# Chunks 4 to 8 cut into columns of 32 tokens, their q loaded by GpSimd during the first unit and turned by VectorE

## The chip, the core and the metric

The kernel runs on one core of a Trainium2 chip. Its parts in this text: TensorE (PE, matmuls; PEld is its weight load), VectorE (DVE), ScalarE (ACT), GpSimd (POOL) and SyncE (SP, which issues DMAs). The metric is the device time of the kernel in microseconds (us): 909.27, the median of three runs (908.77 to 909.46).

## The reference

An attention block without a softmax, then a two-layer block on its output:

```python
kv  = einsum('bhsd,bhse->bhde', k, v)          # 8 batches, 8 heads, 576 tokens, 64 wide
o   = einsum('bhsd,bhde->bhse', q, kv)
x   = o / sqrt(mean(o*o, -1) + 1e-6) * g_norm  # per token and head
x   = x.transpose(0, 2, 1, 3).reshape(4608, 512)
r   = maximum(x @ w_in, 0)                     # 512 -> 2048
out = (s * (r * r) + b) @ w_out                # 2048 -> 512
```

All is float32 but w_in and w_out, which come as 64-bit floats and are made float32 on the chip.

## The kernel before

**Chunks, pairs, units.** The 4608 tokens are cut into 36 chunks of 128 tokens, four chunks make one of nine units of 512 tokens, and from chunk 4 on the attention is worked out for two chunks at a time (c and c+1, c even). A chunk need not be 128 tokens in a row: `parts(c)` (L119) says which. Two cuts exist. In the first nine chunks (two batches) a batch is seen as 64 rows of 9 columns, token = 9p + j, and a chunk is two columns of 64 tokens. In the others a batch is seen as 32 rows of 18 columns, token = 18t + j, and a chunk is four columns of 32 tokens. The output rows follow the same cut: `store` (L1206) issues one DMA for each column, so two for a chunk of the first kind (64 rows) and four for one of the second (32 rows).

**Loading and turning q.** TensorE needs q with the head's 64 numbers on the partitions. For a chunk of the first kind `load_q` (L131) issues two DMAs on the queues it is given (SP in all calls that matter here), which put tokens on the partitions; `turn` (L518) then has TensorE transpose it in four instructions (L534) into PSUM and ScalarE copy it out (L535). For a chunk of the second kind the DMAs themselves bring each 32-token column of each head and half head to its block, 16 DMAs for each run of neighbouring columns, issued by GpSimd (L1623 in the profile); VectorE then turns the 32 x 32 blocks, a whole pair in one instruction (L524), or one chunk of it (L530) where the pair is mixed, as chunks 8 and 9 are. The steps after that are `product` (L545), `back` (L557), `square`, `row_sum`, `norm` (L578), `turn_x` (L589) and `scale`. The q tiles have two buffers, so the load of chunks 8 and 9 goes where chunks 4 and 5 were.

**The order of the work** is written out by hand. In unit 0 twelve plain blocks of the first layer run (`first_unit`, L1633), with the conversion of the weights' 1 MB blocks beside them (`raw` on ScalarE, `convert` on VectorE, three raw buffers); then the fourth part of the layer by a seven-product scheme (`mm1`: x1, z2, x6, y7, x5, x3, y4), then the second layer in 14 slots (`mm2`). The attention of the next unit is put between these: `side_of` (L1590) gives the steps beside the second layer, by slot number, and `sides` (L1680) those beside the first layer; A is the first pair of the next unit, B the second. `at(n)` runs the steps of place n. An engine works through its instructions in the order in which they are written, so a step that waits holds what is written after it on the same engine.

**DMA issue.** SP issues the weights, k and v, and the stores of derived weights to DRAM (`store_w2`, L315). GpSimd issues the output stores, the stores of sums of w_out (L1110) and the q loads of the second kind. `of_w` holds the two halves of `sums_w_in(3)` (L253 and L250): sums of weights that y7, x5 and later products of unit 0 read.

Of the kernel before, what the change touches and what calls it, by code (L numbers as in the profile page):

```python
# [9 lines left out]
FP32 = mybir.dt.float32  # L10
# [6 lines left out]
def kernel(  # L17
# [39 lines left out]
    nc = tc.nc  # L57
# [60 lines left out]

    def parts(c):  # L119

        g, i = divmod(c, R)
        if g == 0:
            if i == 4:
                return [(0, 8, 1), (1, 8, 1)]
            b, i = (0, i) if i < 4 else (1, i - 5)
            return [(b, i, 1), (b, 4 + i, 1)]
        if i == 4:
            return [(2 * g, 16, 2), (2 * g + 1, 0, 2)]
        return [(2 * g, 4 * i, 4)] if i < 4 else [(2 * g + 1, 4 * i - 18, 4)]

    def load_q(c, queues=(nc.sync, nc.sync), rest_on=nc.gpsimd):  # L131

        t = qp.tile([P, 2 * DM], FP32, name="q_sb", tag="q")
        q_tile[c] = t
        pieces = []
        for i in range(2):
            if c + i < R:
                q_in[c + i] = t[:, i * DM : i * DM + DM].rearrange("p (h d) -> p h d", h=H)  # L140
        for s, queue in enumerate(queues):
            for i in range(2):
                if c + i < R:
                    b, j, _ = parts(c + i)[s]
                    queue.dma_start(
                        out=q_in[c + i][s * HB : s * HB + HB],
                        in_=q[b].rearrange("h (p j) d -> p j h d", j=R)[:, j],
                    )
        for i in range(2):
            if c + i < R:  # L150
                continue
            w = 4 * i
            for b, j, n in parts(c + i):
                if pieces and pieces[-1][1] == b and pieces[-1][2] + pieces[-1][3] == j:
                    pieces[-1][3] += n
                else:
                    pieces.append([w, b, j, n])
                w += n
            q_in[c + i] = t.rearrange("p (a w) -> p a w", a=NP)[:, :, i * P : i * P + P]
            if c + i == R:  # L160
                q_in[R] = t[:, DM:].rearrange("p (a w) -> p a w", a=NP)
        rest = []
        for w, b, j, n in pieces:
            src = q[b].rearrange("h (t j) d -> h t j d", j=JC)
            to = t.rearrange("p (a w d) -> p a w d", a=NP, d=32)
            if c < R:
                to, w = t[:, DM:].rearrange("p (a w d) -> p a w d", a=NP, d=32), 0
            for h in range(H):
                for a in range(2):
                    rows = slice(32 * (2 * (h % 2) + a), 32 * (2 * (h % 2) + a) + 32)  # L170
                    rest.append(
                        partial(
                            rest_on.dma_start,
                            out=to[rows, h // 2, w : w + n, :],
                            in_=src[h, :, j : j + n, a * 32 : a * 32 + 32],
                        )
                    )
        return rest
# [319 lines left out]
    def attention_of_two(c):  # L498
# [16 lines left out]
        W = 8  # L515
        st = {}

        def turn(i=None):  # L518
            if i in (None, 0):
                st["qT"] = attp.tile([P, 2 * DM], FP32, name="qT", tag="qT").rearrange(  # L520
                    "p (a x) -> p a x", a=NP
                )
            if i is None:
                nc.vector.transpose(  # L524
                    out=st["qT"], in_=q_tile[c].rearrange("p (a x) -> p a x", a=NP)
                )
                return
            to = st["qT"][:, :, i * P : i * P + P]
            if c + i >= R:
                nc.vector.transpose(out=to, in_=q_in[c + i])  # L530
                return
            ps = ps_t.tile([P, NP, P], FP32, name="qT_ps", tag="t")
            for p in range(NP):
                nc.tensor.transpose(ps[:, p, :], q_in[c + i][:, 2 * p : 2 * p + 2, :], ident)  # L534
            nc.scalar.copy(to, ps)  # L535

        def product():
            ps = [ps_t.tile([P, 2, 2 * P], FP32, name="y_ps", tag="t") for _ in range(2)]
# [123 lines left out]
    def g_s1(s):  # L662
        add(ga["s1", s], ga["a21", s], ga["a22", s])
# [404 lines left out]
    def mm2(u, step=None, side={}):  # L1068
# [135 lines left out]
            return st[name, j]  # L1204

        def store(name, j, c, cols=slice(0, DM), queues=(nc.gpsimd, nc.gpsimd)):  # L1206
            view = out_9 if c < R else out_18
            w = view.shape[2]
            for s, (b, jj) in enumerate((b, jj + i) for b, jj, n in parts(c) for i in range(n)):
                queues[s % 2].dma_start(  # L1210
                    out=view[b, jj, :, cols], in_=st[name, j][s * w : s * w + w, cols]
                )
# [377 lines left out]
    def side_of(A, B, sums, u):  # L1590

        if u == 0:
            return {
                6: [lambda: kv_product(1)],
                7: [partial(A["turn"], 0), partial(A["turn"], 1)],
                8: [A["product"], A["back"], A["square"]],
                9: [A["row_sum"], partial(B["turn"], 0), partial(B["turn"], 1)],
                10: [A["norm"], A["turn_x"], A["scale"], B["product"], B["back"], B["square"]],
                11: [B["row_sum"], B["norm"]],
                12: [B["turn_x"], B["scale"], lambda: [fn() for fn in sums_w_in(0)]],  # L1600
                13: [sums],
            }
        of_w_in = [
            partial(sums_of_w_in, *with_tags)
            for with_tags in zip(DEEP, ((5, 6), (7, 4), (5, 6)))
        ]
        return {
            0: [A["scale"]],
            1: [B["turn"]],
            4: [B["product"], B["back"], B["square"]],  # L1610
            5: [B["row_sum"]],
            6: [B["norm"], of_w_in[1]],
            8: [B["turn_x"], B["scale"], of_w_in[2]],
            11: [sums],
            13: [partial(loads, 3, 1)],
            3: [of_w_in[0]],
        }

    def loads(u, i):

        if u < U:
            for load in load_q(4 * u + 2 * i):
                load()  # L1623

    def raw(i):
        hi(i)
        lo(i)
# [5 lines left out]
    def first_unit():  # L1633
        of_x = x_sums(0)
        of_w = []

        for n, slot in enumerate(slots0):
            if n > 1:
                out_of = slot()
                if out_of:  # L1640
                    out_of()
                if n % 4 == 0:
                    g_s1(n // 4 - 1)
            if 0 < n < 9:
                raw(n + 2)
                convert(n + 2)
            elif n == 0:
                continue
            elif n == 9:
                of_w += sums_w_in(3)  # L1650
                of_w[0]()
            elif n == 10:
                of_x[0]()
                raw(11)
                of_x[1]()
            else:
                of_w[1]()
            if n < 11:
                scale_g()
            if n == 9:  # L1660
                more(8)
        a = mm1(0, NS - 1)
        for fn in (
            a["x1"], scale_g, partial(convert, 11), partial(more, 9),
            a["z2"],
            a["x6"], partial(raw, 12), scale_g, partial(g_s1, 2),
            a["y7"], partial(convert, 12),
            a["x5"], partial(raw, 13), scale_g, partial(more, 10), partial(more, 11),
        ):
            fn()  # L1670
        return a
# [8 lines left out]
    def sides(u, A, B):  # L1680
# [9 lines left out]
        if u == 1:  # L1690
            for s in range(1, NS - 1):
                first[((0, 1), (0, 3))[s - 1]] = list(sums_w_in(s))
            first.update({
                (1, 3): kv,
                (2, 0): [partial(A["turn"], 0), partial(A["turn"], 1)],
                (2, 1): [A["product"]],
                (2, 2): [A["back"]],
                (2, 3): [A["square"]],
                (3, 0): [A["row_sum"]],
                (3, 2): [A["norm"], A["turn_x"]],  # L1700
                (3, 3): [lambda: [load() for load in load_q(12, rest_on=nc.sync)]],
            })
            return first, second
# [39 lines left out]
    for u in range(U):  # L1743
# [38 lines left out]
        for n, slot in enumerate(second):  # L1782
            slot()
            if u == 0:
                if n == 0:
                    convert(13)
                    load_kv(1, 0, convp, tag="raw", bufs=3)
                    store_w2(1, 5)
                    for name in ("x3", "y4", "y4_square"):
                        last[name]()  # L1790
                    raw(14)
# [2 lines left out]
                elif n == 1:  # L1794
                    convert(14)
                    load_kv(1, 1, convp, tag="raw", bufs=3)
                    raw(15)
                    loads(1, 0)
                    loads(1, 1)
                elif n == 2:  # L1800
                    convert(15)
                    t2 = convp.tile([P, 4 * R * D], FP32, name="w_t2", tag="raw", bufs=3)
# [43 lines left out]
```

## Time and profile before

| | |
|---|---|
| median of the three runs | 909.27 us |
| the profiled execution's own time | 909.36 us |
| its span, first to last instruction | 907.6 us |
| TensorE busy | 897.1 us, 99% |
| VectorE busy | 667.2 us, 74% |
| ScalarE busy | 357.5 us, 39% |
| GpSimd busy | 227.6 us, 25% |
| TensorE's waits for another engine or a DMA | 6.5 us, in eleven waits |
| q loads by GpSimd (L1623), issue time | 256, 143.7 us |
| turns by TensorE (L534) | 20, 2.7 us |
| turns of a pair by VectorE (L524) | 13, 1236 ns each |

Times inside the execution count from the span's start. The chain of waits is the path of work that ended last, followed back through what released each step. A timeline lists an engine's instructions with their start, their length and the idle time before them.

### The profile page before, as it was taken

Reading aid. Unit: us, or ns where it says so; the run is one execution under the profiler, and the core shown is the slowest. Engines: PE = TensorE matmul, PEld = TensorE weight load, DVE = VectorE, ACT = ScalarE, POOL = GpSimd, SP = SyncE. Lnnn points to the kernel's source line nnn. Section 1 sums busy time; section 2 is a strip of 40 time slices with the busy share of each in tenths; the row PEclk is TensorE's granted clock in tenths of the full one; section 3 lists DMA queues with packets and bytes.
Section 4 is the critical chain, followed back from the end, with each engine's and each line's share of the span. In section 5 each row is a group of like instructions: output and inputs, shape, how many; then the busy total and the mean of one; then the engine's idle time right before and its main releaser. Section 6 shows DMA issues by size and latency. Waiting matters only on the chain.

```text
span 907.6 us, 19247 instructions
## 1 busy us (share of the span) xinstructions
PE 897.1 (99%) x7514; PEld 824.9 (91%) x7514; DVE 667.2 (74%) x1234; ACT 357.5 (39%) x603; POOL 227.6 (25%) x432
## 2 busy tenths in 40 slices
PE   7999999999999999999999999999999999999998
PEld 7888888888889998999899998999899989999998
DVE  2889576587567986878678857885878777874686
ACT  2887134531148115630365026701680057104710
POOL 2000017014623233811283026503440300021000
PEclk9999999999999999999999999999999999999999
DMA  9695968239943894379626972598438811891285
GB/s 255 221 319 173 280 159 242 84 90 397 334 135 84 282 328 140 79 246 315 188 72 191 308 246 77 128 306 259 126 94 287 287 36 53 278 305 47 56 258 184
DMA packets 120138, 180.34 MB, mean 199 GB/s; under 512 B 29168, under 2 KB 46320, under 8 KB 120048
## 3 DMA queue, kind: packets, MB, share of 16 engines
q1 hardware_dynamic: 101552, 153.00, 53.7%
q0 software_dynamic: 15040, 23.88, 8.8%
q10 hardware_dynamic: 3456, 2.23, 1.0%
q8 instruction: 60, 0.98, 0.4%
q14 instruction: 30, 0.25, 0.1%
HBM read 153.36 MB, written 25.69 MB: 197 GB/s over the span
## 4 chain that ended last, share of the span: by engine, by line
PE 89%; DVE 5%; ACT 2%; DMA 2%; issue 1%; ACTq 0%; DVEq 0%
PE x_ps L91 46%; PE y_ps L91 26%; PE z_ps L91 9%; PE sx_ps L91 4%; PE y_ps L545 2%; DMA kv_sb<-in_v_dram 1%; PE kv_ps L366 1%; DMA w_raw<-in_moe_w_in_dram 1%; ACT w_raw L230 1%; PE z_ps L366 1%; ACT w_raw L225 1%; DVE xs L253 1%; DVE xn L578 0%; DVE a L253 0%; DVE w_up L245 0%
## 5 line engine op out<-in xcount | busy, mean ns | idle before, releaser
L1623 POOL DMA_DIRECT2D q_sb<-in_q_dram x256 | 143.7, 570 | 133.9 <-ACT a L652 62.6
L1210 POOL DMA_DIRECT2D out_dram<-o x110 | 54.8, 505 | 395.8 <-issue 153.0
L91 PE MATMUL x_ps<-w_sb,sub 128*128 128x128 f32 x1176 | 148.8, 275 | 0.6 <-DVE r L250 0.6
L91 PEld LDWEIGHTS x_ps<-w_sb,sub 128*128 128x128 f32 x1176 | 139.7, 192 | 0.9 <-DVE r L250 0.9
L644 ACT ACTIVATE a<-a,b_col,s_col 128x512 f32<-128x512 f32 x144 | 116.2, 813 | 29.6 <-DVE a L647 23.2
L91 PE MATMUL x_ps<-xs,ws 128*128 128x256 f32 x528 | 125.2, 380 | 0.1
L91 PE MATMUL y_ps<-xs,wb 128*128 128x256 f32 x528 | 124.6, 381 | 0.2 <-DVE wb L253 0.2
L91 PEld LDWEIGHTS y_ps<-xs,wb 128*128 128x128 f32 x528 | 97.5, 190 | 13.3 <-issue 0.6
L91 PEld LDWEIGHTS x_ps<-xs,ws 128*128 128x128 f32 x528 | 96.9, 190 | 12.1 <-ACT r L718 0.5
L819 ACT COPY a<-x_ps 128x512 f32<-128x512 f32 x28 | 16.4, 584 | 216.2 <-PE x_ps L91 216.0
L91 PE MATMUL x_ps<-xT,wa 128*128 128x256 f32 x360 | 83.7, 381 | 0.1
L91 PEld LDWEIGHTS x_ps<-xT,wa 128*128 128x128 f32 x360 | 66.7, 190 | 10.3 <-issue 1.5
L250 DVE TENSOR_TENSOR r<-sx_ps,a 128x256 f32<-128x256 f32 x63 | 26.6, 422 | 62.2 <-PE sx_ps L91 62.1
L91 PE MATMUL x_ps<-w_sb,a 128*128 128x128 f32 (+1 forms) x432 | 64.9, 298 | 0.0
L91 PE MATMUL y_ps<-w_sb,a 128*128 128x128 f32 (+1 forms) x416 | 62.1, 295 | 0.0
L91 PEld LDWEIGHTS x_ps<-w_sb,a 128*128 128x128 f32 x432 | 58.9, 191 | 3.3 <-issue 0.4
L91 PEld LDWEIGHTS y_ps<-w_sb,a 128*128 128x128 f32 x416 | 56.1, 192 | 2.1
L250 DVE TENSOR_TENSOR a<-y_ps,r 128x512 f32<-128x512 f32 x38 | 26.1, 688 | 37.7 <-PE y_ps L91 30.0
L250 DVE TENSOR_TENSOR r<-x_ps,o 128x256 f32<-128x256 f32 (+1 forms) x84 | 29.7, 353 | 29.3 <-PE x_ps L91 28.6
L91 PE MATMUL y_ps<-w_sb,sub 128*128 128x128 f32 x392 | 49.5, 275 | 0.0
L253 DVE TENSOR_TENSOR a<-a,a 128x512 f32<-128x512 f32 x72 | 46.8, 684 | 0.4
L91 PE MATMUL z_ps<-w_sb,a 128*128 128x128 f32 (+1 forms) x352 | 46.8, 280 | 0.0
(185 smaller groups left out, 1519.6 us busy)
## 6 DMA issues: line engine op xcount, KB each, us to landing
w_sb<-w SPq DMA_DIRECT2D x385, 256.0 KB, 4.4
w_raw<-in_moe_w_in_dram SPq DMA_DIRECT2D x8, 1024.0 KB, 7.8
w_raw<-in_moe_w_out_dram SPq DMA_DIRECT2D x8, 1024.0 KB, 5.0
w_sb<-w SPq DMA_DIRECT2D x14, 512.0 KB, 8.8
w<-sub POOLq DMA_DIRECT2D x28, 256.0 KB, 6.5
w_sb<-in_k_dram SPq DMA_DIRECT2D x24, 288.0 KB, 4.8
w_sb<-in_v_dram SPq DMA_DIRECT2D x24, 288.0 KB, 5.0
out_dram<-o POOLq DMA_DIRECT2D x92, 64.0 KB, 4.0
```

The lines of the kernel that those rows point to most:

```text
L91: nc.tensor.matmul(o, lhsT=lhsT, rhs=rhs, start=start, stop=stop, skip_group_check=True)
L225: nc.scalar.activation(hi, hi, AF.Prelu, scale=2.0**-112, alpha=-(2.0**32))
L230: nc.scalar.activation(lo, lo, AF.Copy, scale=2.0**-29)
L250: nc.vector.tensor_tensor(out=o, in0=a, in1=b, op=ALU.add)
L253: nc.vector.tensor_tensor(out=o, in0=a, in1=b, op=ALU.subtract)
L366: nc.tensor.matmul(ps[r][(r ^ l) * HB : (r ^ l) * HB + HB, i, :], lhsT=kv[l][0][rows, j, :], rhs=kv[l][1][rows, j, :], start=(j == 0), sto ...
L545: nc.tensor.matmul(ps[l][32 * p : 32 * p + 32, r, lo:hi], lhsT=bd_kv[b % 2][rows, p, at : at + 32], rhs=st["qT"][rows, p, lo:hi], start=Tr ...
L644: nc.scalar.activation(t, t, AF.Identity, scale=s_col, bias=b_col)
L819: nc.scalar.copy(g_tile("a11", s), st["x", s])
L1210: queues[s % 2].dma_start(out=view[b, jj, :, cols], in_=st[name, j][s * w : s * w + w, cols])
L1623: load()
```

## The change

Only chunks 0 to 3 keep the first cut. Chunks 4 to 8 get columns of 32: chunk 4 is columns 8 and 17 of batch 0 and columns 0 and 1 of batch 1; chunks 5 to 8 are columns 2 to 17 of batch 1. Which batch a token of a pair belongs to, and so the runs of `product`, stay as they were. `turn` loses the path over TensorE and ScalarE: each pair is turned by VectorE in one instruction.

The loads of chunks 4 to 7 leave SP, where they were issued in slot 1 of the second layer of unit 0. GpSimd issues them from block 4 of the first unit on, behind a copy of one column that waits for that block's sum (`g_s1(0)`). The turn of A moves one slot forward. `of_w[1]` is written ahead of block 11 in place of behind it, and the store of two derived weights moves from slot 0 to slot 1, behind the second load of k and v of batch 1.

```diff
     def parts(c):
+        if c < 4:
+            return [(0, c, 1), (0, 4 + c, 1)]
+        if c == 4:
+            return [(0, 8, 1), (0, 17, 1), (1, 0, 2)]
         g, i = divmod(c, R)
         if g == 0:
-            if i == 4:
-                return [(0, 8, 1), (1, 8, 1)]
-            b, i = (0, i) if i < 4 else (1, i - 5)
-            return [(b, i, 1), (b, 4 + i, 1)]
+            return [(1, 4 * i - 18, 4)]
...
-        def turn(i=None):
...
-            ps = ps_t.tile([P, NP, P], FP32, name="qT_ps", tag="t")
-            for p in range(NP):
-                nc.tensor.transpose(ps[:, p, :], q_in[c + i][:, 2 * p : 2 * p + 2, :], ident)
-            nc.scalar.copy(to, ps)
+        def turn():
+            st["qT"] = attp.tile([P, 2 * DM], FP32, name="qT", tag="qT").rearrange(
+                "p (a x) -> p a x", a=NP
+            )
+            nc.vector.transpose(
+                out=st["qT"], in_=q_tile[c].rearrange("p (a x) -> p a x", a=NP)
+            )
...
-            view = out_9 if c < R else out_18
+            view = out_9 if c < 4 else out_18
...
-                6: [lambda: kv_product(1)],
-                7: [partial(A["turn"], 0), partial(A["turn"], 1)],
+                6: [A["turn"], lambda: kv_product(1)],
                 8: [A["product"], A["back"], A["square"]],
-                9: [A["row_sum"], partial(B["turn"], 0), partial(B["turn"], 1)],
+                9: [A["row_sum"], B["turn"]],
...
         for n, slot in enumerate(slots0):
+            if n == 11:
+                of_w[1]()
             if n > 1:
                 out_of = slot()
...
+                if n == 4:
+                    t = small("begin", 1)
+                    nc.gpsimd.tensor_copy(out=t, in_=ga["s1", 0][:, 0, :1])
+                    loads(1, 0)
+                    loads(1, 1)
...
-            else:
-                of_w[1]()
...
-                (2, 0): [partial(A["turn"], 0), partial(A["turn"], 1)],
+                (2, 0): [A["turn"]],
                 (2, 1): [A["product"]],
...
                     load_kv(1, 0, convp, tag="raw", bufs=3)
-                    store_w2(1, 5)
...
                     load_kv(1, 1, convp, tag="raw", bufs=3)
+                    store_w2(1, 5)
                     raw(15)
-                    loads(1, 0)
-                    loads(1, 1)
```

More of the change, by code (lines that the diff above doesn't have):

```diff
@@ L136, in load_q @@
         q_tile[c] = t
-        pieces = []
-        for i in range(2):
-            if c + i < R:
+        if c < 4:
+            for i in range(2):
                 q_in[c + i] = t[:, i * DM : i * DM + DM].rearrange("p (h d) -> p h d", h=H)
-        for s, queue in enumerate(queues):
-            for i in range(2):
-                if c + i < R:
+            for s, queue in enumerate(queues):
+                for i in range(2):
                     b, j, _ = parts(c + i)[s]
@@ L148, in load_q @@
                     )
[L149 to L155, printed above, removed]
-                else:
[L157 to L161, printed above, removed]
+            return []
+        pieces, w = [], 0
+        for b, j, n in parts(c) + parts(c + 1):
+            if pieces and pieces[-1][1] == b and pieces[-1][2] + pieces[-1][3] == j:
+                pieces[-1][3] += n
+            else:
+                pieces.append([w, b, j, n])
+            w += n
         rest = []
@@ L165, in load_q @@
             to = t.rearrange("p (a w d) -> p a w d", a=NP, d=32)
-            if c < R:
-                to, w = t[:, DM:].rearrange("p (a w d) -> p a w d", a=NP, d=32), 0
             for h in range(H):
@@ L516, in attention_of_two @@
         st = {}
-        def turn(i=None):
[L519 to L531, printed above, removed]
-            ps = ps_t.tile([P, NP, P], FP32, name="qT_ps", tag="t")
-            for p in range(NP):
-                nc.tensor.transpose(ps[:, p, :], q_in[c + i][:, 2 * p : 2 * p + 2, :], ident)
-            nc.scalar.copy(to, ps)
+        def turn():
[5 more added lines that the diff above has]
+            )
         def product():
@@ L1655, in first_unit @@
                 of_x[1]()
-            else:
-                of_w[1]()
             if n < 11:
```

## The prediction

> **What bounds the kernel now.** I read the page's busy times and its chain first.
>
> ```profile
> PE 897.1 (99%) x7514; PEld 824.9 (91%) x7514; DVE 667.2 (74%) x1234; ACT 357.5 (39%) x603; POOL 227.6 (25%) x432
> PE 89%; DVE 5%; ACT 2%; DMA 2%; issue 1%; ACTq 0%; DVEq 0%
> ```
>
> TensorE never rests, and its waits sum to 6.5 us. So an instruction taken from TensorE is worth its length if no wait takes its place, and work elsewhere counts only where TensorE comes to wait for it. The chain of waits in time prices what goes:
>
> ```profile
> 109.81 0.87 PE qT_ps L534 x8
> 118.98 0.87 PE qT_ps L534 x8
> ...
> 158.47 0.44 PE qT_ps L534 x4
> ```
>
> The rest is slack, read in timelines: of VectorE and TensorE about the turn of chunks 8 and 9 (unit 1),
>
> ```profile
> 159.85 0.69 DVE L647 SCALAR_TENSOR_TENSOR a<-a 128x512 f32<-128x512 f32 x1
> 160.46 0.71 DVE L530 STREAM_TRANSPOSE qT<-q_sb 128x512 f32<-128x512 f32 x1
> ...
> 162.20 1.89 PE L91 MATMUL z_ps<-xT,wa 128*128 128x256 f32 x8
> 164.02 1.16 PE L545 MATMUL y_ps<-qT,bd_kv 64*32 64x128 f32 x64
> ```
>
> of the queues that feed this turn,
>
> ```profile
> 138.16 3.27 POOL L1623 DMA_DIRECT2D q_sb<-in_q_dram  x6 [0.19 <-issue]
> 142.48 0.55 POOL L1623 DMA_DIRECT2D q_sb<-in_q_dram  x1 [1.04 <-DMA out_dram<-o]
> ...
> 152.38 8.04 POOL L1623 DMA_DIRECT2D q_sb<-in_q_dram  x14 [0.34 <-DMA q_sb<-in_q_dram]
> ...
> 155.39 3.57 SPq L1046 DMA_DIRECT2D w_sb<-w  x4
> ```
>
> and of the place where the four parts of the first layer meet in unit 0:
>
> ```profile
> 71.87 0.81 ACT L644 ACTIVATE a<-a,b_col,s_col 128x512 f32<-128x512 f32 x1 [1.83 <-DVE a L691]
> 72.59 0.56 ACT L718 COPY r<-x_ps 128x512 f32<-128x512 f32 x1
> ...
> 72.58 1.97 PE L91 MATMUL y_ps<-xs,wb 128*128 128x256 f32 x8 [0.23 <-DVE wb L253]
> 74.39 1.89 PE L91 MATMUL x_ps<-xs,ws 128*128 128x256 f32 x8
> ```
>
> [...] the trace has 272 ns a transpose, four in 0.44 us, and a 585 ns copy. [...] the trace has 1236 ns for a pair. [...] the eight q loads issued from 150.2 to 155.2 landed in 2.0 us (median), the nine after them, beside SP's four 512 KB loads, in 5.7. [...]
>
> **The change, part by part,** against the profiled span, 907.6 us (the execution took 909.36, so 1.8 lie around the span; the median is 909.27). I put the differences on the median.
>
> 1. Turns off TensorE: 0.87 + 0.87 + 0.44 = **-2.18 us**. Five copies (585 ns) leave ScalarE, on no path.
>
> 2. Turns on VectorE: two more of 1.24 us and one that grows from 0.71. A's turn falls after the sum at 105.64, where VectorE idles 4.19 us; TensorE wants it at 114. B's falls behind the row sum that ends at 120.6, with 2.78 us idle. Cost 0; without that cover 1.24 us each would shift the attention steps behind it.
>
> 3. q of chunks 4 to 7 by GpSimd: chunk 4 has three runs of columns (48 loads), chunks 6 and 7 one (16). These 64 start after the sum at 47.5 to 48.1. Around 140 to 160, with DMA engines 97% busy for most of it, 32 loads took 22.3 us, 0.70 each; 64 take 45 us and end near 93. A needs its 48 at 105.5, B the rest at 120. Cover: 12 us and more; it is gone at 1.2 us a load. GpSimd has nothing else until its stores at 124. They bring 1 MB to DMA engines that are 87% busy from 46 to 70, where ScalarE waits for weight blocks (0.2 to 1.0 us each). Blocks may slip by 0 to 0.3 us; VectorE reads them later in turn, so I take 0.
>
> 4. SP loses eight q loads, and `store_w2(1, 5)` goes behind the loads of k and v. These, which landed shortly before TensorE needed them at 103.8, come earlier; the stores, some 4 us later, have to be read before VectorE overwrites w_up at 100.8: three us of slack by my count. 0.
>
> 5. `of_w[1]` first. y7 (72.58) no longer waits 0.23 us. But block 11's relu and square (L686, L691) now stand 1.2 us later on VectorE; ScalarE's affine of that block waits for the square (1.83 us already), and behind it is the copy r (L718, 72.59) without which x5 (74.39) can't add to its bank. The copy ends near 74.3 in place of 73.1, and x5 starts where it did. Gain 0, loss up to 0.1: **+0.07**.
>
> 6. The turn of chunks 8 and 9 in unit 1. Before, its VectorE half needed 16 GpSimd loads, landed by 154. Now it needs 32, all in GpSimd's queue behind the last output stores. In the times of before (all shifts alike until here): TensorE reaches the product at 164.09 - 0.44 = 163.65, so the turn must start by 162.3 and the last load land by 162.2. [...] the first 20 crawl while the engines are full. Upper bound: the 32nd load lands like the 32nd of before (issued 159.8, 5.7 to 6.2 to landing, so 165.9): a wait of 3.7. Lower: loads 17 to 32 issue-bound at 0.55 and landed in 2.0: 158.1 + 2.0 = 160.1, no wait. Between: SP's two q loads of 128 KB are gone, so the engines drain about 1.5 us earlier, near 150; loads 17 to 20 follow at the pace of landings to 151.3, 12 more at 0.55 put the 32nd at 157.8. SP's four loads start at 155.4, and the loads of before issued then landed at 163 to 163.5. Wait 1.1, restart 0.1: **+1.2 us** (0 to 3.7). Behind the turn on VectorE stand z2's sum and square, whose readers come 5 us later.
>
> 7. Output stores of chunks 4 to 7: 16 in place of 8, half the size, in front of unit 2's q loads (L1623 at 241 to 254). These already hold VectorE:
>
> ```profile
> 259.63 1.25 DVE L524 STREAM_TRANSPOSE qT<-q_sb 128x1024 f32<-128x1024 f32 x1 [1.86 <-DMA q_sb<-in_q_dram]
> 260.80 0.65 DVE L250 TENSOR_TENSOR a<-y_ps,a 128x512 f32<-128x512 f32 x1
> ...
> 264.12 1.89 PE L91 MATMUL y_ps<-xs,wb 128*128 128x256 f32 x8
> ```
>
> The y4 at 264.12 adds to the bank that the sum at 260.80 reads, ended by 261.45: slack 2.67 us. Eight more issues of 0.54 are 4.3 us, of which the pauses at the head of the q loads take up some: they come 0.4 to 2.5 us later. 0, with an allowance of **+0.1**.
>
> Sum: -2.18 + 0.07 + 1.2 + 0.1 = -0.8: span 906.8, time **908.5**.
>
> **The rivals.** *No wait* (0.30): the loads run at issue pace, and 6 comes to its lower bound. For it: the page's landings of 2.0 us; against: the 5.7 beside SP's loads. Time 909.27 - 2.18 + 0.07 = 907.2.
>
> *The stores push the turn in unit 2* (0.17), slower. If each of the eight extra stores costs the eighth part of a landing (6.6 us in that stretch, so 0.83), the loads come 6.6 us later, 3.9 past the slack: 909.27 - 2.18 + 0.07 + 1.2 + 3.9 = 912.3. It costs from 2.67 us on and decides at about 5.4. For it: GpSimd is nearly full from 227 to 254; against: the stores are half as large, and the pauses absorb.
>
> That the change doesn't do what it says I exclude: the 20 turns plainly go.
>
> **How the numbers follow.** Wait in unit 1: 0.53, time 908.5, own range 907.5 to 909.9. A measurement of this kernel tells about 0.2% (1.8 us) from no change, so this case is no change, no wait is just faster, the stores are slower. Faster 0.30, within 0.2% 0.53, slower 0.17. The range goes from 906.9, under the no-wait case, to 911.0, a wait at its upper bound; what is outside is most of the third case.
>
> **What would show it.** No L534 on TensorE; in unit 0 no TensorE wait at the products of L545; x5 of unit 0 preceded by the ScalarE copy L718; L524 in unit 1 with idle time released by a q load, and behind it a TensorE wait of about 1 us at L545; in unit 2 a longer idle before L524 but y4 on time. I am wrong if GpSimd's loads in the first unit take over 1.2 us each, if the weights' blocks slip by more than a few tenths, or if the 32nd load lands before 162 or after 166 on the clock of before.

## The result, and the profile after

The changed kernel took 912.31 us (median of 20 runs) against 909.65 us of the kernel before on the same chip: ratio 1.0031, 95% interval 1.0023 to 1.0039, so 2.7 us slower. The forecast was 908.5, and its range ended at 911.0. One of the kernel before's 20 runs took 1888.52 us and is left out of the ratio.

The profiled execution took 916.24 us (span 914.5), the slowest of the 20, so its waits may be larger than those of a middle one; what belongs to this execution alone has to be told apart below. The page's busy times and the head of its chain, after:

```profile
PE 898.0 (98%) x7494; PEld 824.3 (90%) x7494; DVE 670.1 (73%) x1236; ACT 355.5 (39%) x598; POOL 276.8 (30%) x523
PE 75%; DMA 8%; issue 7%; DVE 6%; POOL 3%; ACT 1%; ACTq 0%; DVEq 0%; POOLq 0%
```

TensorE has its 20 turns less (7,494 instructions, before 7,514), yet is busy 0.9 us longer: others took longer. And the chain now runs through DMAs and GpSimd. Lines moved: the product is L526, VectorE's turn L514, the copy r L699, GpSimd's q loads L1603. The view of TensorE's waits (engine, tile, line, what it waited for: sum, times, longest):

```profile
PE y_ps L526 <- DVE qT L514: 3.3, 1, 3.3
PE x_ps L91 <- ACT r L699: 2.2, 2, 1.6
...
PE y_ps L91 <- DVE a L242: 0.4, 1, 0.4
```

None of the three was in the kernel before, where y7's 0.23 us stood in place of the second. The timelines give their places (start, length, then in brackets the idle time before and what ended it). In **unit 0**, TensorE waits in front of x6 and x5, and the second layer starts at 78.31, 2.2 us later than before (76.11):

```profile
72.14 1.99 PE L91 MATMUL x_ps<-xs,ws 128*128 128x256 f32 x8 [1.57 <-ACT r L699]
73.97 1.89 PE L91 MATMUL y_ps<-xs,wb 128*128 128x256 f32 x8
76.47 1.99 PE L91 MATMUL x_ps<-xs,ws 128*128 128x256 f32 x8 [0.62 <-ACT r L699]
78.31 3.62 PE L91 MATMUL x_ps<-w_up,a 128*128 128x256 f32 x16
```

Followed back, this is ScalarE's work on the weights' 1 MB blocks, which had not arrived:

```profile
55.04 1.15 ACT L217 ACTIVATE w_raw<-w_raw 128x1024 f32<-128x1024 f32 x1 [0.25 <-DMA w_raw<-in_moe_w_out_dram]
...
59.44 1.14 ACT L217 ACTIVATE w_raw<-w_raw 128x1024 f32<-128x1024 f32 x1 [1.50 <-DMA w_raw<-in_moe_w_out_dram]
```

In **unit 1** the turn waits 5.00 us for q, and TensorE waits for the turn (the timelines of VectorE and of TensorE):

```profile
165.98 1.25 DVE L514 STREAM_TRANSPOSE qT<-q_sb 128x1024 f32<-128x1024 f32 x1 [5.00 <-DMA q_sb<-in_q_dram]
...
162.21 1.89 PE L91 MATMUL z_ps<-xT,wa 128*128 128x256 f32 x8
167.38 1.96 PE L526 MATMUL y_ps<-qT,bd_kv 64*32 64x128 f32 x64 [3.28 <-DVE qT L514]
169.27 3.78 PE L91 MATMUL y_ps<-xs,wb 128*128 128x256 f32 x8
```

After the wait the product takes 1.96 us where it took 1.16, and the y4 after it 3.78 in place of 1.89. The table by stretch shows why (stretch in us, its length, busy time and instructions of PE, PEld, DVE, ACT, POOL; then the granted clock, the DMA share and GB/s): for 6.82 us, from inside the wait on, TensorE had half its clock.

```profile
160.00:166.51 6.51, 4.10 (x19) 3.25 (x18) 1.48 (x3) 3.32 (x5) 2.17 (x4) 1.00 0.88 265
166.51:173.33 6.82, 5.96 (x74) 4.79 (x75) 2.23 (x4) 0.81 (x1) 5.80 (x11) 0.50 0.27 57
173.33:176.00 2.67, 2.67 (x14) 2.36 (x13) 2.60 (x5) 1.28 (x2) 0.00 (x0) 1.00 0.00 1
```

From 167.38 to 173.33 TensorE worked 5.95 us at half speed, 3.0 us more than the work needs: the wait of 3.28 cost 6.3. The 20 runs differ in this clock. By the mean clock of a run:

| mean clock | runs | median, us |
|---|---|---|
| 1.0 | 3 | 910.51 |
| 0.998 | 9 | 911.81 |
| 0.997 | 5 | 913.31 |
| 0.996 | 3 | 915.06 |

In the profiled execution, one of those at 0.996, the half clock lasted 6.82 us. A mean of 0.998 over 912 us is a loss of some 1.8 us of full clock, an estimate from the mean; the profile of the kernel with `of_w[1]` behind block 11 (below), which has this mean, shows 3.41 us at half. The table doesn't part the clock from the wait, since in these two profiles the longer wait came with the longer stretch at half clock (2.61 us with 3.41, 3.28 with 6.82). Nor does it tell 0.997 from 0.998: the mean takes in the last microseconds, in which TensorE has nothing left to do (in the profiled execution its last instruction ends at 910.59, and from 914.0 to 914.5 the clock is 0.53). On the waits that came with half the clock, see the last section.

In **unit 2** the turn waits 5.05 us for q (1.86 before), and the sum behind it holds y4 for 0.41 us:

```profile
268.97 1.25 DVE L514 STREAM_TRANSPOSE qT<-q_sb 128x1024 f32<-128x1024 f32 x1 [5.05 <-DMA q_sb<-in_q_dram]
270.14 0.65 DVE L242 TENSOR_TENSOR a<-y_ps,a 128x512 f32<-128x512 f32 x1
...
270.85 1.99 PE L91 MATMUL y_ps<-xs,wb 128*128 128x256 f32 x8 [0.41 <-DVE a L242]
```

Against the span before (+6.9): +2.2 in unit 0, -2.18 for the turns, +6.3 in unit 1, +0.4 in unit 2, 6.7 in all. Two theories for the loss follow: *unit 1*, a turn that comes late and then halves the clock; *unit 0*, GpSimd's loads, which slow the weights' blocks. The rival to each is that the other does it.

### The profile page after: what moved, and what is told of

Same layout as the page of the kernel before. It is cut to its first block, busy times and chain, and to the rows that moved or that the text cites. A ratio compares the mean times of both kernels' runs of the same rounds, so it can differ in the third digit from the quotient of the medians.

```text
span 914.5 us, 19293 instructions
## 1 busy us (share of the span) xinstructions
PE 898.0 (98%) x7494; PEld 824.3 (90%) x7494; DVE 670.1 (73%) x1236; ACT 355.5 (39%) x598; POOL 276.8 (30%) x523
## 4 chain that ended last, share of the span: by engine, by line
PE 75%; DMA 8%; issue 7%; DVE 6%; POOL 3%; ACT 1%; ACTq 0%; DVEq 0%; POOLq 0%
PE x_ps L91 38%; PE y_ps L91 22%; PE z_ps L91 8%; PE sx_ps L91 4%; DMA q_sb<-in_q_dram 3%; PE y_ps L526 2%; DMA w<-sub 1%; POOL q_sb L1603 1%; DMA out_dram<-o 1%; DMA kv_sb<-in_v_dram 1%; POOL w L1091 1%; DMA w_raw<-in_moe_w_in_dram 1%; DMA w_raw<-in_moe_w_out_dram 1%; PE z_ps L358 1%; DVE xn L559 0%
## 5 line engine op out<-in xcount | busy, mean ns | idle before, releaser
L1603 POOL DMA_DIRECT2D q_sb<-in_q_dram x336 | 188.3, 568 | 143.8 <-ACT a L633 62.9
L1191 POOL DMA_DIRECT2D out_dram<-o x120 | 59.3, 501 | 314.6 <-issue 152.1
```

The source lines that it names most:

```text
L1191: queues[s % 2].dma_start(out=view[b, jj, :, cols], in_=st[name, j][s * w : s * w + w, cols])
```

## The experiments

All ratios are to the kernel before, measured on the same chip. They are estimates from the single runs and not quotients of two medians; where a kernel has few runs (five for the two with unit 2's turn later) the two differ by up to 0.07%. "Changed" means the changed kernel.

| kernel | median us | ratio | 95% interval |
|---|---|---|---|
| changed | 912.31 | 1.0031 | 1.0023 to 1.0039 |
| unit 1's turn two places later | 909.0 | 0.9991 | 0.9983 to 0.9999 |
| loads from block 8 on | 911.29 | 1.0021 | 1.0011 to 1.0031 |
| `of_w[1]` behind block 11 | 912.14 | 1.0023 | 1.0010 to 1.0036 |
| later turn, later loads | 909.09 | 0.9993 | 0.9986 to 1.0000 |
| before, q loads added | 922.32 | 1.0139 | 1.0120 to 1.0159 |
| later turn, no q loads | 909.26 | 0.9995 | 0.9987 to 1.0004 |
| before, turn repeated 7 times | 912.12 | 1.0025 | 1.0017 to 1.0032 |
| before, turn repeated 10 times | 915.86 | 1.0064 | 1.0051 to 1.0076 |
| SP's loads after the turn | 907.68 | 0.9976 | 0.9966 to 0.9986 |
| and unit 2's turn later | 907.30 | 0.9964 | 0.9952 to 0.9977 |
| and `of_w[1]` behind block 11 | 907.23 | 0.9966 | 0.9952 to 0.9979 |
| before, 32 q loads added | 910.09 | 1.0003 | 0.9995 to 1.0011 |

### Unit 1's turn two places later

```diff
-                (2, 0): [A["turn"]],
-                (2, 1): [A["product"]],
-                (2, 2): [A["back"]],
-                (2, 3): [A["square"]],
-                (3, 0): [A["row_sum"]],
+                (2, 2): [A["turn"]],
+                (2, 3): [A["product"]],
+                (3, 0): [A["back"], A["square"]],
+                (3, 1): [A["row_sum"]],
```

> The changed kernel, with the turn and the product of chunks 8 and 9 two places later in unit 1 (back, square and row sum follow, norm stays), so that the 32 loads have some 3.5 us more to land. Theory 1, the wait at this product and the halved TensorE clock behind it are most of the loss: both go, the mean clock is 1.0, and against before there remain -2.2 (turns) + 2.2 (first unit) + 0.4 (unit 2), so about +0.4 us, ratio 1.0004. Rival, the wait only shows what another place costs (weights late in unit 0, VectorE fuller): TensorE waits elsewhere for as long and the ratio stays near 1.003.

909.0 us, ratio 0.9991. In TensorE's timeline the product waits 0.63 us, for the turn's place behind other VectorE work and no longer for q, and the matmuls around it show no half clock (the product takes 1.15 us, those behind it 1.99 and 1.89; the execution's mean clock is 0.999):

```profile
169.21 1.15 PE L526 MATMUL y_ps<-qT,bd_kv 64*32 64x128 f32 x64 [0.63 <-DVE qT L514]
```

Set against the changed kernel's ratio, 0.40% or 3.6 us come back (0.11% either way, from the two intervals), so unit 1 is the whole loss of 0.31%, as far as the noise allows. It is even better than theory 1 had it (1.0004): the 2.2 us that theory took over from unit 0 of the profiled execution don't show in the times.

### The loads in the first unit from block 8 on

```diff
-                if n == 4:
+                if n == 8:
                     t = small("begin", 1)
-                    nc.gpsimd.tensor_copy(out=t, in_=ga["s1", 0][:, 0, :1])
+                    nc.gpsimd.tensor_copy(out=t, in_=ga["s1", 1][:, 0, :1])
```

> The changed kernel, with GpSimd's 64 loads of the first unit started from block 8 in place of block 4 (some 14 us later), when most weight blocks are in. Theory 2, these loads slow the weight blocks' transfers by about 2.5 us each and so cost 2.2 us at x6 and x5: ScalarE's waits for w_raw between 54 and 60 us shrink to those of before, the 1.57 us wait at x6 goes, x5 waits at most 0.1; the wait in unit 1 stays. About 2.0 us less than the changed kernel: ratio near 1.001. Rival, of_w[1] ahead of block 11 is what delays x6 and x5: no gain, 1.003.

911.29 us, ratio 1.0021, between the theory's 1.001 and the rival's 1.003: if anything 0.1% better than the changed kernel, with intervals that overlap. Its profile turned the question. GpSimd's first load is issued at 64.58, and yet ScalarE waited for the same weight block before that:

```profile
59.00 1.17 ACT L217 ACTIVATE w_raw<-w_raw 128x1024 f32<-128x1024 f32 x1 [1.17 <-DMA w_raw<-in_moe_w_out_dram]
```

So blocks can come late without GpSimd's loads, and a third possibility joined: they come late in some executions whatever GpSimd does.

### `of_w[1]` behind block 11, as before

```diff
-            if n == 11:
-                of_w[1]()
...
+            else:
+                of_w[1]()
```

> The changed kernel with of_w[1] behind block 11 again, as before the change. Theory 2 (late weight blocks): x6 still waits 1.6 us; y7 waits some 0.5 us for wb in place of x5's 0.6 for the copy; no difference, ratio 1.003. Rival (the order is to blame): x6 and x5 start as before, 2 us less, ratio 1.001.

912.14 us, ratio 1.0023. x5 no longer waits, y7 waits in its place:

```profile
73.69 1.97 PE L91 MATMUL y_ps<-xs,wb 128*128 128x256 f32 x8 [0.49 <-DVE wb L245]
75.50 1.89 PE L91 MATMUL x_ps<-xs,ws 128*128 128x256 f32 x8
```

The time doesn't tell the two orders apart: one wait for another.

### Both: later turn and later loads

The edits of the first two kernels together.

> The changed kernel with both edits, the later turn in unit 1 and the loads from block 8. If the two waits are all of the loss: 909.65 - 2.18 (turns) + 0.07 (x5) + 0.4 (unit 2) = 907.9, ratio 0.998, clock 1.0. If a third cost hides (the stores in unit 2, VectorE's added turns), the ratio is 1.0 or above.

909.09 us, ratio 0.9993, the same as with the later turn alone. Where unit 1 is out of the way, the place of GpSimd's loads in the first unit makes no difference that can be measured. The 907.9 us that were to stand if the two waits were all of the loss are missed by over 1 us; 0.6 of that is the product's wait for the later turn, and what the rest is remains open.

### Before, with the q loads added

```diff
+                if n == 4:
+                    t = small("begin", 1)
+                    nc.gpsimd.tensor_copy(out=t, in_=ga["s1", 0][:, 0, :1])
+                    for pieces in (
+                        [(0, 0, 8, 1), (1, 0, 17, 1), (2, 1, 0, 2), (4, 1, 2, 4)],
+                        [(0, 1, 6, 4), (4, 1, 10, 4)],
+                    ):
+                        t = qp.tile([P, 2 * DM], FP32, name="q_spare", tag="q")
...
+                                    nc.gpsimd.dma_start(
+                                        out=to[lo : lo + 32, h // 2, w : w + m, :],
+                                        in_=src[h, :, j : j + m, c2 * 32 : c2 * 32 + 32],
+                                    )
```

> The kernel before with GpSimd's 64 loads of q added in the first unit from block 4 on, into the two q buffers that are free then; nothing reads them, and SP still loads q itself later. The two last runs of 16 loads are three columns shorter or as long as in the changed kernel. Theory 'GpSimd's loads slow the weight blocks' (read from the profile of the changed kernel, where mm2 of unit 0 began 2.2 us late): TensorE waits for some 2 us in front of blocks 6 and 5 of the first layer, 911.6 us, ratio 1.0022. Rival 'the blocks come late in some executions whatever GpSimd does' (read from the kernel whose loads begin at block 8 and whose weights were late before any of them): no difference, 909.6 us, ratio 1.000, no wait of over 0.3 us there.

922.32 us, which neither theory had, and the kernel is at fault: runs of six and eight columns were split in two, so it has 96 loads and not 64, GpSimd issues them until 112, and SP's own load of q for chunks 6 and 7 has to wait for those into the same buffer. Behind that load in SP's queue is the store of a derived weight (`w_dn`), which is issued at 116.95 only; VectorE waits for it before it overwrites this weight, and behind this on VectorE stands the `back` (L557) for which TensorE's next turn waits (VectorE's timeline, then the view of TensorE's waits):

```profile
126.19 2.50 DVE L253 TENSOR_TENSOR w_dn<-w_dn,w_t 128x512 f32<-128x512 f32 x4 [13.78 <-DMA w<-w_dn]
...
PE qT_ps L534 <- DVE q_sb L557: 11.4, 1, 11.4
```

So the time says nothing. The first unit comes before all this and can be read: with GpSimd issuing from 49.15 on, ScalarE takes the weight blocks without a wait, they land as evenly as in the most even of the other profiles (4.9 to 5.1 there; here the line of the block loads, issue to landing), and the second layer starts at 75.45.

```profile
DMA to landing us min/median/max: 5.1/5.2/5.2
```

### Later turn, no q loads

As the kernel with unit 1's turn two places later, with

```diff
-                    loads(1, 0)
-                    loads(1, 1)
+                    for c in (4, 6):
+                        q_tile[c] = qp.tile([P, 2 * DM], FP32, name="q_sb", tag="q")
+                        nc.gpsimd.memset(q_tile[c], 1.0)
```

> The changed kernel with unit 1's turn two places later and without the loads of q for chunks 4 to 7: GpSimd fills the two tiles with ones instead, so the output of these chunks is not the reference's. To be compared with the same kernel with the loads (909.0 us, ratio 0.9991). Theory 'GpSimd's loads slow the weight blocks': x6 and x5 of unit 0 come up to 1.3 us earlier and only the 0.6 us wait that comes from the order on VectorE stays in front of x5: 908.0 us, ratio 0.998. Rival 'late in some executions anyway': 909.0 us, ratio 0.999.

909.26 us, ratio 0.9995 (the same kernel with the loads: 0.9991). Taking all 64 loads away gains nothing; by the two intervals they cost at most 0.1%. And in the profile of this kernel, in which GpSimd loads nothing at that time, x6 waits 0.41 us and x5 0.59 all the same.

### Before, 32 q loads added

The same question without the collision: only the first two runs of the list, 32 loads, of which the last is issued by 69.5.

```diff
+                    for pieces in ([(0, 0, 8, 1), (1, 0, 17, 1)],):
```

> The kernel before with only the first 32 of GpSimd's loads of q added in the first unit (single columns, 4 KB each), into a buffer that is free then and that nothing reads; SP's own loads of q come later than these have landed. Theory 'GpSimd's loads slow the weight blocks': blocks land up to 2.5 us later and TensorE waits in front of x6 and x5: 911.6 us, ratio 1.002. Rival 'the blocks come late in some executions whatever GpSimd does': 909.7 us, ratio 1.000, and blocks that land as fast as in the kernel before.

910.09 us, ratio 1.0003 (0.9995 to 1.0011): the 2 us (1.0022) are excluded, no cost at all is not. From block 4 to the second layer, TensorE's only wait in its profile is that of y7, 0.50 in place of 0.23.

The six profiles without these loads (in two of them they begin in the last three microseconds of the window) and the eight with them show how much the blocks differ by themselves. Median time from issue to landing, blocks issued from 44 to 66, us:

| | |
|---|---|
| with GpSimd's loads | 7.8 (changed), 5.7, 7.3, 5.2, 6.6, 5.2, 6.4, 6.4 |
| without | 5.3 (before), 6.7, 5.2, 5.3, 5.3, 5.0 |

The middle values are 6.4 and 5.3, so the loads may well lengthen the landings; but both groups hold slow and even ones, and the changed kernel's profile is the extreme. That TensorE pays for it in the median of many runs is not shown.

### Before, VectorE's turn of chunk 9 repeated

A wait of a chosen length at the product of unit 1, with no DMA in it: seven and ten repetitions.

```diff
-                (2, 0): [partial(A["turn"], 0), partial(A["turn"], 1)],
+                (2, 0): [partial(A["turn"], 0)] + [partial(A["turn"], 1)] * 8,
```

(11 in place of 8 for ten.)

> The kernel before, with the turn of chunk 9 on VectorE in unit 1 done seven times more than needed (0.62 us each), so that TensorE waits some 1.5 us in front of the product of chunks 8 and 9. Theory 'a long wait also halves TensorE's clock, a short one does not': a wait of 1.4 to 1.6 us, the clock stays at 1.0, 911.1 us, ratio 1.0016. Rival 'a wait costs its length only': the same here.

> As the one with seven repetitions, with ten: TensorE waits some 3.4 us in front of the same product. Theory 'a long wait also halves the clock': [...] which costs 1 to 3 us more than the wait: 914 to 916 us, ratio 1.005 to 1.007. Rival 'a wait costs its length only': 913.0 us, ratio 1.0037, clock 1.0 throughout.

Seven: a wait of 1.76 us, clock 1.0 in the profile, +2.3 us (0.25%, interval 0.17 to 0.32), which is the wait within the noise:

```profile
166.63 0.67 PE L545 MATMUL y_ps<-qT,bd_kv 64*32 64x128 f32 x32 [1.76 <-DVE qT L530]
```

Ten: a wait of 3.99 us and

```profile
167.81 1.11 PE L545 MATMUL y_ps<-qT,bd_kv 64*32 64x128 f32 x32 [3.99 <-DVE qT L530]
168.85 3.78 PE L91 MATMUL y_ps<-xs,wb 128*128 128x256 f32 x8
```

the matmuls after it at half speed again, with the granted clock at 0.50 from 166.0 to 172.0 (0.95 in the 2 us before, 0.92 in the 4 us after, so from about 165.8 to 172.6 by my estimate), and +5.8 us (0.64%, interval 0.51 to 0.76). In the profile, the 4.8 us of work at half speed are 2.4 more than the work needs. The waits differ by 2.2 us, the times by 3.5 (1.3 either way). A cost of the wait alone would have put ten at 909.74 + 4.0 = 913.7, ratio 1.0044, below the interval. All five runs of ten had a mean clock of 0.998 or 0.996; of the 16 runs of seven, three had 0.998 and none less. So the halved clock is a cost of its own, in a kernel in which nothing else of the change was made.

### SP's loads held back until the turn

Of the 32 q loads in unit 1, the last landed 7.7 us after its issue, while four 512 KB loads by SP, issued from 155.84 on, were under way. What they bring is used at 190. Here a copy of one column into their buffer, behind the turn on VectorE, holds them back:

```diff
+        def begin_w():
+            nc.vector.tensor_copy(out=late["ring"][:, next_at[0], :1], in_=q_tile[8][:, :1])
...
-                (1, 3): kv,
+                (1, 3): kv[:1],
                 (2, 0): [A["turn"]],
-                (2, 1): [A["product"]],
+                (2, 1): [A["product"], begin_w, kv[1]],
```

> The changed kernel, with SP's four 512 KB loads into the ring (issued from 155.8 on in the changed kernel, needed at 190 only) held back until VectorE has turned chunks 8 and 9: one small VectorE copy into the ring after the turn. Nothing else is moved. Theory 'SP's four loads make the last q loads late, and this alone makes TensorE wait': the 32nd q load lands some 2 us after its issue instead of 6.5 to 7.7, no wait of over 0.3 us at the product of unit 1, clock 1.0 throughout, and what stays of the loss is the 0.6 us in front of x5 of unit 0 and 0.4 to 0.8 us in unit 2: 908.4 us, ratio 0.9986. Rival 'GpSimd's loads are late by their own pace': a wait of 2 to 3 us stays, 912 us, ratio 1.003.

907.68 us, ratio 0.9976. The issues of q loads by GpSimd between 156 and 159, from issue to landing, in the changed kernel:

```profile
DMA to landing us min/median/max: 1.9/5.8/7.7
```

and with SP's loads held back:

```profile
DMA to landing us min/median/max: 2.0/2.4/3.4
```

The turn starts at 160.05, SP's loads at 164.91, and TensorE meets its q:

```profile
161.34 1.89 PE L91 MATMUL z_ps<-xT,wa 128*128 128x256 f32 x8
163.16 1.16 PE L526 MATMUL y_ps<-qT,bd_kv 64*32 64x128 f32 x64
164.25 1.99 PE L91 MATMUL y_ps<-xs,wb 128*128 128x256 f32 x8
```

One small copy is worth 0.55% against the changed kernel (1.0031 less 0.9976; with both intervals 0.13% either way), 5.0 us with 1.2 either way. (The profile is that of the slowest of its nine runs, 909.77 us.)

### And unit 2's turn two places later

```diff
-                4: [A["turn"]],
                 5: kv,
+                6: [A["turn"]],
                 8: [A["product"]],
```

> The kernel that holds SP's loads back, and the turn of chunks 12 and 13 in unit 2 two places later (slot 6 in place of 4), so that the sum behind it on VectorE no longer waits for q. Theory 'the 0.4 to 0.8 us in front of y4 of unit 2 come from the turn that waits for q ahead of a sum': this wait is gone, 0.4 to 0.8 us less than without it: 907.8 us, ratio 0.998. Rival 'the product at slot 8 then waits instead': no gain, 908.4 us.

907.30 us, ratio 0.9964. The wait of y4 is 0.31 us in this profile, 1.03 in the one before it:

```profile
261.78 1.99 PE L91 MATMUL y_ps<-xs,wb 128*128 128x256 f32 x8 [0.31 <-DVE a L242]
```

That is 0.7 less between these two executions, the first of which is the slowest of its kernel's, and no wait came at the product in slot 8; the two ratios' intervals overlap, so the times don't settle how much of it stays over many runs.

### And `of_w[1]` behind block 11

The edit of the third kernel on top.

> As the kernel with SP's loads held back and unit 2's turn later, and also the sums of_w[1] behind block 11 as in the kernel before. Theory 'the order on VectorE in unit 0 only exchanges x5's wait for y7's': 0.6 us in front of x5 go, 0.25 to 0.5 in front of y7 come, 907.6 us, within 0.05% of the kernel with of_w[1] first. Rival 'the new order was right by itself': 0.3 us or more slower than it.

907.23 us, ratio 0.9966: no difference from `of_w[1]` first. The x5 wait of 0.6 that this edit was to take away is absent from the profile of the kernel with `of_w[1]` first, too; y7's wait came (0.49). Both orders of this kernel beat the kernel before by about 0.35% (0.2 to 0.5 by the intervals) and the changed one by about 0.65%.

## Why the prediction was wrong

**Step 1, the turns (-2.18): the runs agree.** With SP's loads held back, and so without the wait in unit 1, the kernel is 0.24% faster than before: 2.2 us, with 0.9 either way. No run has the turns alone taken away. The two kernels with unit 2's turn later gain 3.2 us; whether that is more than the turns give, and from where, the runs don't tell.

**Step 6, the turn of chunks 8 and 9 (+1.2): the path right, the size wrong, and this is the failure.** TensorE did wait for this turn, the turn for the last q loads, and these were late beside SP's four loads, as worked out. Two things were wrong: how late they landed, and what the wait costs. The 32nd load was issued at 158.21, which is the forecast 157.8, an estimate, on the clock of before: unit 1 stands 0.45 us later (product wanted at 164.10 against 163.65). The landing was taken from loads of before issued at that time, 163 to 163.5; it came at 165.9, 165.45 on that clock, 7.7 us after its issue where some 5.5 had been assumed (6.5 in the kernel with the later turn; why the executions differ is open). The wait was 3.28 where 1.1 stood, near the upper bound of 3.7. The prediction's own sign of being wrong, a landing after 166 on the clock of before, did not come; the range of landings held, and the price put on it did not. The bound of 3.7 priced the wait, and not what a wait of that length does to TensorE's clock, for which neither the sum nor the bounds had a term: 3.0 us more in the profiled execution. In the median the whole is 5.0 where 1.2 stood. The three runs whose clock stayed at 1.0 give an estimate of its parts: at 910.51 us they lie 3.2 above what the kernel before (909.5 without its one far run) less the turns would take, so some 3 of the 5.0 are the wait and some 2 the clock. The term was missing because the trace of before shows a clock of 1.0 throughout: its longest wait is 1.5 us, and no idle time of this length was there to show the fall.

**Step 3, GpSimd's loads in the first unit (0): right as far as the times tell.** 32 of the loads on the kernel before cost 0.03% (at most 0.11%), and without any of the 64 the later-turn kernel is no faster. GpSimd took 45.5 us over the 64 (49.21 to 94.75), as estimated. The 2.2 us of the profiled execution, which by the prediction's own words ("if the weights' blocks slip by more than a few tenths") would have put this step in the wrong, come from blocks that were late in this execution. My first reading of the two profiles, that the loads cost this, has fallen. Why blocks land in 5 us in one profile and in over 7 in another is open; that the loads have a part in it is not excluded.

**Step 5, `of_w[1]` first (+0.07).** The place was right: x5 waits for the copy r. The size was 0.6 in six of the seven profiles with this order and nothing in the seventh (unit 2's turn later), and y7's 0.23 to 0.5 is what it replaces; the times show no difference.

**Steps 2 and 4 (0): right.** No product of unit 0 waits for its turn, and the loads and stores that SP issues in the second layer cause no wait on TensorE that wasn't there before.

**Step 7, the stores in front of unit 2's turn (+0.1).** The longer idle before the turn came (5.05 after 1.86), and used up the slack of 2.67 us: y4 waits 0.4 in the changed kernel, 1.0 in the one with SP's loads held back, where 0.1 had been allowed. That is the mechanism of the slower rival at a small part of its 3.9 us. Its 912.3 us agree with the 912.31 measured by chance: the loss sat in unit 1.

The sum for the median: -2.2 for the turns, +5.0 for unit 1, +2.8 against 2.7 measured. This is no check of its own: the 5.0 are the distance to the kernel with SP's loads held back, and the sum closes because that kernel gained just what the turns were to give. It says that steps 3, 5 and 7 together cost about nothing, with 0.9 us either way.

## What to carry to other kernels

A late transfer on an engine that never rests is not priced by the wait alone: where the upper bound comes near two or three microseconds, add what TensorE loses at half its clock afterwards (here waits of 2.61 and 3.28 us came with 3.41 and 6.82 us of it). Before small loads with a near deadline are put behind each other, look at what another queue starts in the same microseconds and when that is needed; here four loads that were needed 34 us after their issue made those late that were needed in five, and holding them back by 9 us was worth more than twice what the change had taken off TensorE. And a difference between two profiles is a difference between two executions: a kernel that has the suspected cause alone, timed over many runs, tells them apart.

## What the runs showed of the hardware

- **Waits of 2.61 us and more in unit 1 came with half the clock.** Those of 2.61, 3.03, 3.28 and 3.99 us did; one of 1.76 didn't in its profile (a clock of 1.00 in every stretch from 164 to 176). In the kernel with `of_w[1]` behind block 11, the wait of 2.61 ended at 165.62 and the half clock began at 167.16, when TensorE was at work again. It lasted 3.41 us:

```profile
164.00:167.16 3.16, 1.54 (x66) 1.35 (x67) 2.51 (x3) 0.35 (x1) 0.80 (x2) 1.00 0.18 53
167.16:170.57 3.41, 3.41 (x10) 2.70 (x9) 0.47 (x1) 0.47 (x1) 3.41 (x7) 0.50 0.26 56
170.57:173.00 2.43, 2.43 (x12) 2.14 (x12) 2.36 (x5) 1.28 (x2) 2.13 (x4) 1.00 0.28 61
```

With the wait of 3.28 it began inside the wait and lasted 6.82 us, with that of 3.99 some 6.8. With that of 3.03 (loads from block 8 on) it shows in the lengths, 1.96 us for the product and 3.78 for the y4 behind it, and in the execution's mean clock of 0.996; the execution with the wait of 11.4 (before, q loads added) has a mean of 0.994. What decides whether the clock falls, and for how long, these runs don't show: three of the 16 runs with seven repetitions had a mean of 0.998 as well.

- **Small loads of GpSimd beside large ones of SP.** The q loads issued between 156 and 159 landed in 2.4 us (median) without SP's four loads of 512 KB and in 5.8, at most 7.7, beside them.

- **1 MB weight blocks** at the same place of these kernels landed in 5.0 to 7.8 us (medians by profile; 5.0 to 6.7 without GpSimd's loads beside them), and the second layer began between 75.2 and 78.3.
